# A fused attention, router, expert and dense kernel: routing chains interleaved, branch hints, one exit branch

## Chip, cores and metric

The kernel runs on one core of a Trainium2 chip. The metric is the device time of one execution in microseconds (us). Beside it stands one execution taken by the hardware profiler, whose trace gives every duration here. TensorE (PE in the rows; PEld is its weight load), VectorE (DVE), ScalarE (ACT), GpSimd (POOL) and SyncE (SP) each run their own list of instructions in order; a "q" behind a name (PEldq, ACTq) is that engine's sequencer with its branches, semaphores and register loads.

## What is computed

```python
# attention with pooled queries: b=4, h=8, 1152 keys of 64; 576 queries, each the mean of two
scores = scale * q_pool @ k^T;  p = exp(scores - max);  x = (p / sum(p)) @ v      # x: 2304 x 512
# routed experts: 8, top-1, for tokens whose skip score is above 0
do_compute = x @ w_skip > 0
e_idx = argmax(xc @ w_gate);  gate_w = softmax(xc @ w_gate)[e_idx]
for e in range(8):
    y[e_idx == e] = gate_w * (relu(xc @ w1[e]) @ w2[e])       # 512 -> 1024 -> 512
x[do_compute] += y
# dense layer, 512 -> 2048 -> 512
h = x @ w_in;  out = (h - tanh(h)) @ w_out
```

With the inputs used, four of the eight experts get tokens, 618, 476, 56 and 2 of them.

## The kernel before

**Stages.** Attention runs to about 449 us, the routing of the last tokens to about 467, the expert stage to about 640, and the dense layer fills the rest. Nothing is reordered by a scheduler: each engine runs its instructions in the order in which the code issues them.

**Routing** (`Router.route`). The tokens lie in 18 tiles of 128 (NT); the first 13 are counted during the attention, and `route` finishes the last five. On VectorE it issues three chains of small operations, one behind the other. The first, lines 652 to 668, counts tokens per expert (`n`), turns them into tiles of 128 slots (`nt`), ranks the experts by tokens (`rnk`, `mt`) and writes `perm`, a table by rank: number of tiles, expert, first slot tile. Lines 669 to 677 then work out `last` (the last slot tile), `few` (whether dense weights are left to load because experts have few tiles) and `more`, which holds for each rank its number of tiles, plus 2NT if the next rank has none. The second chain, `rank` (lines 600 to 611), gives each token its place within its expert. The third, lines 682 to 685, adds the expert's first slot and writes `sg16`, an f16 copy. `invert` compares `sg16` with slot numbers and multiplies on TensorE, which gives `inv`, the token that stands in each slot; the first gather of tokens (`fetch`, line 845, an indirect transfer issued by GpSimd) reads it. The first expert's weights (`load`, line 836, also GpSimd) need only `perm`, which the engine reads into registers (`reg`, line 819; the register load is called TENSOR_LOAD).

**Experts** (`Experts`). The counts are known on the chip only, so the code holds for rank a as many copies of a tile as it could need: 18, 9, 6, 5, 4, 3, 3, 3. `place(a)` stands in `If(n > 0)` (line 938), runs tile 0, then `chain(1)`, in which each further tile is nested in `If(n > j)` (line 945), then `place(a + 1)`. So every engine meets one compare per tile, and behind an expert's last tile each jumps over the copies that are left. On the side that is not taken it adds the semaphore counts which the skipped instructions would have added (EVENT_SEMAPHORE rows; INC_SWDGE_SEM on GpSimd), and goes on. With these inputs ranks 0 to 3 have 5, 4, 1 and 1 tiles and ranks 4 to 7 none. Behind rank 3 the engines therefore jump twice: out of its chain (line 945) and over `place(4)` (line 938).

**A tile** (`tile(a, j, base)`). TensorE multiplies 96 times into the hidden layer (line 889, 128x128), transposes the next tile's tokens (line 865), and multiplies 24 times back (128x512). ScalarE and VectorE split float32 into f16 pairs (lines 850, 851), make the hidden activations (904, 905); ScalarE copies the result of the tile before (`evac`, line 869), GpSimd stores it (874) and gathers the next tokens (845). In an expert's last tile `If(self.end <= j + 1)` (line 925) splits the first part of the next expert's weights; `self.end` is `more` in a register of ScalarE and VectorE. Behind the stage stand `dense.fetch_y` (line 1024, two gathers by GpSimd), the last `evac` and `store`, and `dense.first` (line 1041).

**Zeros.** The rows `ys` that hold the experts' results are filled with zeros during the attention, by six transfers on SyncE's queue: five of 1280 KB and one of 256 KB, in `on_pair`.

Of the kernel before, what the change touches and what calls it, by code (L numbers as in the profile page):

```python
# [13 lines left out]
I32 = mybir.dt.int32  # L14
# [475 lines left out]
class Router:  # L490
# [4 lines left out]
    def __init__(self, ctx, tc, w_skip, w_gate, x_all, ident32, ov):  # L495
# [8 lines left out]
        self.r7, self.slot, self.inv = t("r7", [P, 2, NT]), t("slot", [P, NT], I32), t("inv", [P, CAP + 2], I32)  # L504
        self.more, self.perm = t("more", [P, 2, E], I32), t("perm", [P, 3, E], I32)
        self.cnt, self.gate, self.last, self.least = t("cnt", [P, E]), t("gate", [P, NT]), t("last", [P, 1]), t("least", [P, E])
        self.iom, self.iota, self.tv = t("iom", [P, 1, E]), t("iota", [P, 1, P]), t("tv", [P, NT])
# [128 lines left out]
    def route(self, ps_pool, tag):  # L636
        nc, e = self.nc, self.EARLY
        T = lambda n, s, dt=F32: self.wk1.tile(s, dt, name=n)
        V = nc.vector
        S88 = [P, E, E]  # L640
        for f in self.pick(e, NT):
            f()
        before, all_ = self.count(e, NT, ps_pool.tile([P, 512], F32, tag=tag, name="ps_r"))
        n, n1 = T("n", [P, E]), T("n1", [P, E], I32)
        key, rk, base = T("key", [P, E]), T("rnk", [P, E]), T("base", [P, E])
        vals = T("vals", [P, 3, 1, E], I32)
        perm = T("permf", [P, 3, E])
        cmp, bt, mt, mm = T("cmp", S88), T("bt", S88), T("mt", S88), T("mm", [P, 3, E, E])
        few, last, so, sl = T("few", [P, 1]), self.last, T("so", [P, NT, E]), T("sl", [P, NT])
        iota8 = self.iota[:, 0, 0:E]  # L650
        nt = vals[:, 0, 0]
        V.tensor_copy(vals[:, 1, 0], iota8)
        V.tensor_tensor(out=n, in0=all_, in1=self.cnt, op=ALU.add)
        V.tensor_scalar(out=n1, in0=n, scalar1=float(P - 1), scalar2=None, op0=ALU.add)
        V.scalar_tensor_tensor(out=key, in0=n, scalar=float(E), in1=iota8, op0=ALU.mult, op1=ALU.subtract)
        V.tensor_scalar(out=nt, in0=n1, scalar1=7, scalar2=None, op0=ALU.logical_shift_right)
        V.tensor_tensor(out=cmp, in0=key.unsqueeze(1).to_broadcast(S88), in1=key.unsqueeze(2).to_broadcast(S88),
                        op=ALU.is_gt)
        V.tensor_tensor(out=bt, in0=cmp, in1=nt.unsqueeze(1).to_broadcast(S88), op=ALU.mult)
        V.tensor_reduce(out=rk, in_=cmp, axis=AX.X, op=ALU.add)  # L660
        V.tensor_reduce(out=base, in_=bt, axis=AX.X, op=ALU.add)
        V.tensor_tensor(out=mt, in0=rk.unsqueeze(1).to_broadcast(S88), in1=iota8.unsqueeze(2).to_broadcast(S88),
                        op=ALU.is_equal)
        V.tensor_copy(vals[:, 2, 0], base)
        V.tensor_tensor(out=mm, in0=vals.to_broadcast([P, 3, E, E]), in1=mt.unsqueeze(1).to_broadcast([P, 3, E, E]),
                        op=ALU.mult)
        V.tensor_reduce(out=perm, in_=mm, axis=AX.X, op=ALU.add)
        V.tensor_copy(self.perm, perm)
        V.tensor_reduce(out=last, in_=nt, axis=AX.X, op=ALU.add)
        V.tensor_tensor(out=perm[:, 1], in0=perm[:, 0], in1=self.least, op=ALU.is_lt)  # L670
        V.tensor_scalar(out=perm[:, 2, 0:E - 1], in0=perm[:, 0, 1:E], scalar1=0.0, scalar2=2.0 * NT,
                        op0=ALU.is_equal, op1=ALU.mult)
        V.tensor_reduce(out=few, in_=perm[:, 1], axis=AX.X, op=ALU.max)
        V.tensor_tensor(out=self.more[:, 1, 0:E - 1], in0=perm[:, 0, 0:E - 1], in1=perm[:, 2, 0:E - 1], op=ALU.add)
        V.tensor_scalar(out=last, in0=last, scalar1=1.0, scalar2=1.0, op0=ALU.max, op1=ALU.subtract)
        V.tensor_copy(self.more[:, 0, 1:2], few)
        V.tensor_copy(self.more[:, 0, 0:1], last)
        for f in self.rank(e, NT, before):
            f()
        for t in range(e, e + 3):  # L680
            self.row(t)
        V.tensor_tensor(out=so, in0=base.unsqueeze(1).to_broadcast([P, NT, E]), in1=self.oh, op=ALU.mult)
        V.tensor_reduce(out=sl, in_=so, axis=AX.X, op=ALU.add)
        V.tensor_tensor(out=self.r7[:, 1], in0=self.r7[:, 1], in1=sl, op=ALU.add)
        V.tensor_copy(self.sg16, self.r7[:, 1])

# [39 lines left out]
class Wide:  # L726
# [43 lines left out]
    def parts(self, i):  # L770
# [7 lines left out]
        else:  # L778
            nc.scalar.copy(dh, a)
        nc.gpsimd.tensor_tensor(out=dl, in0=a, in1=dh if dh.dtype == F16 else dh.bitcast(F32), op=ALU.subtract)  # L780


class Experts:
# [381 lines left out]
def pooled_attention__moe__tanhshrink_kernel(ctx, tc, q, k, v, moe_w_skip, moe_w_gate, moe_w1, moe_w2,  # L1165
# [8 lines left out]
    with tc.manual_schedule():  # L1174
# [7 lines left out]
        with ExitStack() as actx:  # L1182
# [5 lines left out]
            def on_pair(b, c):  # L1188
# [10 lines left out]
                if b == 0:  # L1199
                    for i in range(c, 6, 4):  # L1200
                        n = 5 if i < 5 else 1
                        todo.append(lambda i=i, n=n: nc.sync.dma_start(
                            out=ys[i * 5 * P:(i * 5 + n) * P].rearrange("(a p) d -> p a d", p=P),
                            in_=zero.unsqueeze(1).to_broadcast([P, n, DM])))
                return todo
# [12 lines left out]
        with ExitStack() as bctx:  # L1218
# [47 lines left out]
```

## Time and profile before

| | us |
|---|---|
| median of 3 runs | 1045.09 (1044.58 to 1046.73) |
| the profiled execution | 1046.08 |
| its span, first to last instruction | 1044.6 |
| TensorE busy in the span | 941.9 (90%) |
| VectorE, ScalarE, GpSimd busy | 788.5, 641.4, 557.1 |
| granted clock of TensorE, mean | 0.962 of full |

The 1.5 us between the profiled execution and its span lie around the instructions. Times within the kernel are counted from the span's start. Busy time is that of computing and data-moving instructions; a branch or a register load is not busy, but has rows of its own, in which its duration holds whatever it waited for. Idle time in brackets stands ahead of an instruction, with what ended it.

### The profile page before, as it was taken

How to read it: one execution, taken by the hardware profiler on the slowest of the kernel's cores; microseconds unless marked ns; L12 is line 12 of the kernel's file. 1: busy time of each engine (PE TensorE's matmuls, PEld its weight loads, DVE VectorE, ACT ScalarE, POOL GpSimd, SP SyncE). 2: the span in 40 equal slices, each digit the busy share in tenths (PEclk: the TensorE clock that was granted, in tenths of full speed). 3: DMA queues.
4: the chain of work that ended last, by engine and by line, in shares of the span. 5: the costliest groups of instructions: out<-in, count | busy, mean ns of one | idle time of the engine just before them, and what ended most of it. 6: DMA issues, size and time to landing. Idle time of an engine off the chain costs nothing. (4 is left out here: it accounts for less than half of the span.)

```text
span 1044.6 us, 25445 instructions
## 1 busy us (share of the span) xinstructions
PE 941.9 (90%) x10249; PEld 704.6 (67%) x10249; DVE 788.5 (75%) x1420; ACT 641.4 (61%) x1211; POOL 557.1 (53%) x491
## 2 busy tenths in 40 slices
PE   5689999999999999939878775999999999999998
PEld 2355666666666666637656543778888888888886
DVE  8678889888889998768979762867666666666654
ACT  4587999888999998835463451444444444444443
POOL 8847998888899986524646411342332223322221
PEclk8889999999999999969989887999999999999999
DMA  7765878666666720169657433121111211212100
GB/s 222 147 157 177 213 190 206 139 134 126 162 143 127 166 59 15 28 224 330 215 180 261 150 126 136 31 72 41 46 56 31 72 41 46 56 32 71 21 21 21
DMA packets 129796, 122.52 MB, mean 117 GB/s; under 512 B 92270, under 2 KB 96878, under 8 KB 128622
## 3 DMA queue, kind: packets, MB, share of 16 engines
q1 hardware_dynamic: 121934, 92.74, 34.7%
q0 software_dynamic: 7712, 27.79, 7.9%
q8 instruction: 92, 1.51, 0.6%
q14 instruction: 58, 0.48, 0.1%
HBM read 74.73 MB, written 19.14 MB: 90 GB/s over the span
## 5 line engine op out<-in xcount | busy, mean ns | idle before, releaser
L242 POOL TENSOR_TENSOR pl<-p,ph 128x512 f16<-128x512 f32 x214 | 263.8, 1252 | 59.5 <-ACT p L237 45.1
L188 DVE TENSOR_REDUCE m<-ps_m 128x1 f32<-128x384 f32 x432 | 225.5, 548 | 37.4 <-PE ps_m L187 34.7
L1095 POOL TENSOR_TENSOR gl<-v,gh 128x512 fp32r<-128x512 f32 x71 | 92.9, 1308 | 270.7 <-ACT gh L1094 268.3
L236 ACT ACTIVATE ph<-ps_e 128x512 f16<-128x512 f32 x279 | 177.0, 635 | 57.5 <-PE ps_e L248 54.2
L299 PEld LDWEIGHTS <-ph 128*128 128x128 f16 x2304 | 133.4, 99 | 49.7 <-issue 22.6
L1094 ACT CAST gh<-v 128x512 fp32r<-128x512 f32 x72 | 44.5, 619 | 188.5 <-DVE v L1093 188.5
L1078 PE MATMUL ps_ch<-xT,wi 128*128 128x256 f16 x576 | 158.7, 275 | 0.7 <-ACT xT L1062 0.7
L1079 PE MATMUL ps_ch<-xT,wi 128*128 128x256 f16 x576 | 157.9, 274 | 1.1 <-DMA xT<-xs 0.8
L1080 PE MATMUL ps_ch<-xT,wi 128*128 128x256 f16 x576 | 157.9, 274 | 0.0
L187 PE MATMUL ps_m<-ks,qT 128*128 128x384 f16 (+1 forms) x480 | 122.7, 338 | 23.9 <-DVE m L188 16.1
L299 PE MATMUL ps_a<-vh,ph 128*128 128x65 f16 x1152 | 136.7, 195 | 0.0
L299 PE MATMUL ps_a<-vh,pl 128*128 128x65 f16 x1152 | 136.6, 195 | 0.0
L299 PE MATMUL ps_a<-vl,ph 128*128 128x65 f16 x1152 | 136.5, 195 | 0.0
L1089 DVE SCALAR_TENSOR_TENSOR v<-u,ps_ch 128x512 f32<-128x512 f32 x72 | 49.3, 685 | 114.4 <-ACT t L1087 108.9
L237 ACT ACTIVATE p<-ps_e 128x512 f32<-128x512 f32 x211 | 134.5, 637 | 0.0
L1111 PE MATMUL ps_co<-wo,gh 128*128 128x512 f32 x288 | 119.7, 416 | 0.0
L1113 PE MATMUL ps_co<-wo,gl 128*128 128x512 f32 x288 | 113.7, 395 | 1.5 <-POOL gl L1095 1.5
L247 PE MATMUL ps_e<-qT,ks 128*128 128x512 f16 x288 | 111.4, 387 | 2.6 <-DVE pl L242 1.8
L1112 PE MATMUL ps_co<-wo,gh 128*128 128x512 f32 x288 | 113.5, 394 | 0.0
L248 PE MATMUL ps_e<-qT,kh 65*128 65x512 f16 x288 | 111.8, 388 | 1.9 <-DMA qT<-mt 1.9
L299 PEld LDWEIGHTS <-pl 128*128 128x128 f16 x1152 | 108.4, 98 | 0.0
L187 PEld LDWEIGHTS <-qT 128*128 128x128 f16 (+1 forms) x480 | 42.9, 102 | 68.1 <-issue 34.3
(222 smaller groups left out, 2152.8 us busy)
## 6 DMA issues: line engine op xcount, KB each, us to landing
v<-in_v_dram SPq DMA_DIRECT2D x16, 576.0 KB
k<-in_k_dram SPq DMA_DIRECT2D x15, 576.0 KB
q<-in_q_dram SPq DMA_DIRECT2D x16, 512.0 KB
raw<-in_moe_w_in_dram SPq DMA_DIRECT2D x8, 1024.0 KB
w1f<-in_moe_w_dram POOLq DMA_DIRECT2D x8, 1024.0 KB, 7.6
w2f<-in_moe_w_dram POOLq DMA_DIRECT2D x8, 1024.0 KB, 8.3
raw<-in_moe_w_out_dram SPq DMA_DIRECT2D x8, 1024.0 KB
ys<-zero SPq DMA_DIRECT2D x5, 1280.0 KB
```

The costliest lines, as they stand in the source:

```text
L187: nc.tensor.matmul(ps[o, 0:384], w, ks[:, h, c * 384:(c + 1) * 384], start=True, stop=True)
L188: nc.vector.tensor_reduce(out=s["m2"][:, i, c:c + 1], in_=ps[:, 0:384], axis=AX.X, op=ALU.max)
L236: nc.scalar.activation(ph, ps, AF.Exp, scale=2.0 ** -20)
L237: nc.scalar.activation(src, ps, AF.Exp, scale=2.0 ** -20)
L242: (nc.vector if dve else nc.gpsimd).tensor_tensor(out=pl, in0=src, in1=ph, op=ALU.subtract)
L299: self.nc.tensor.matmul(o, x, r, start=first and i == 0, stop=k == NKT - 1 and i == 2, skip_group_check=True)
L1078: nc.tensor.matmul(ps[:, a], self.wi[0][:, w], xh[:, c], start=c == 0, stop=False)
L1079: nc.tensor.matmul(ps[:, a], self.wi[0][:, w], xl[:, c], start=False, stop=False)
L1080: nc.tensor.matmul(ps[:, a], self.wi[1][:, w], xh[:, c], start=False, stop=c == 3)
L1111: nc.tensor.matmul(o, gh[:, a, s], self.wo[0][:, w], start=f == 0, stop=False)
L1112: nc.tensor.matmul(o, gh[:, a, s], self.wo[1][:, w], start=False, stop=False)
L1113: nc.tensor.matmul(o, gl[:, a, s], self.wo[0][:, w], start=False, stop=f == 15)
```

## The change

Four things change. In `route`, the three chains become lists of operations, and the first two are issued in turn, one of each; the last step of the first chain (`mm`, `permf`, `perm`) is issued in turn with the third. The eight operations for `last`, `few` and `more` become `tails`, issued behind `invert`. The 256 KB of zeros are issued by GpSimd behind the attention. In the expert stage `tile` issues, where the expert may have one more tile, a hint to all engines on whether `n > j + 1`, tied to the branch of that tile by a label; one more hint goes to the branch on `few` behind the stage. And `self.end` is loaded by all five engines, with a new `If(self.end != 2 * NT + 1)` around `chain(1)` and `place(a + 1)`: it is not entered where the expert has one tile and the next has none.

```diff
@@ Router.route
+        place = [
+            lambda: V.tensor_tensor(out=n, in0=all_, in1=self.cnt, op=ALU.add),
...
+            lambda: V.tensor_copy(vals[:, 2, 0], base)]
+        order = [
+            lambda: V.tensor_tensor(out=mm, in0=vals.to_broadcast([P, 3, E, E]),
...
+            lambda: V.tensor_copy(self.perm, perm)]
+        slots = [
+            lambda: V.tensor_tensor(out=so, in0=base.unsqueeze(1).to_broadcast([P, NT, E]), in1=self.oh, op=ALU.mult),
...
+            lambda: V.tensor_copy(self.sg16, self.r7[:, 1])]
...
+        rank = self.rank(e, NT, before)
+        for i, f in enumerate(place):
+            f()
+            if i < len(rank):
+                rank[i]()
...
+        for i, f in enumerate(slots):
+            f()
+            if i < len(order):
+                order[i]()
+
+    def tails(self):
...
-        for f in self.rank(e, NT, before):
-            f()
@@ Experts
-    def tile(self, a, j, base):
+    def tile(self, a, j, base, n):
         nc = self.nc
+        if j + 1 < self.MOST[a]:
+            self.tc.mark_branch_hint_location("t%d_%d" % (a, j + 1), hint=n > j + 1, engines=ALL)
...
-                self.end = self.reg(self.more[:, 1], a, 3 * NT, (T.Activation, T.DVE))
+                self.end = self.reg(self.more[:, 1], a, 3 * NT, ALL)
...
-                    with tc.If(n > j):
-                        self.tile(a, j, base)
+                    with tc.If(n > j, label="t%d_%d" % (a, j)):
+                        self.tile(a, j, base, n)
                         chain(j + 1)
-            self.tile(a, 0, base)
-            chain(1)
-            self.place(a + 1)
+            self.tile(a, 0, base, n)
+            with tc.If(self.end != 2 * NT + 1) if a + 1 < E else ExitStack():
+                chain(1)
+                self.place(a + 1)
...
+        self.tc.mark_branch_hint_location("few", hint=few, engines=T)
...
-        with self.tc.If(few > 0):
+        with self.tc.If(few > 0, label="few"):
@@ on_pair, behind att.run() and behind invert
-                    for i in range(c, 6, 4):
-                        n = 5 if i < 5 else 1
+                    for i in range(c, 5, 4):
...
+            nc.gpsimd.dma_start(out=ys[25 * P:26 * P], in_=zero)
             router.route(att.ps_mx, "mx")
...
             router.invert(ps_i)
+            router.tails()
```

**VectorE, in `route`, from the copy of perm on, before.** Line 668 writes the table that GpSimd loads; 669 to 677 are the eight operations on `last`, `few` and `more`; 600 to 604 begin `rank`.

```order
L668 CAST perm<-permf 128x24
L669 TENSOR_REDUCE last<-vals 128x1
L670 TENSOR_TENSOR permf<-permf,least 128x8
L671 TENSOR_SCALAR permf<-permf 128x7
L673 TENSOR_REDUCE few<-permf 128x1
L674 TENSOR_TENSOR more<-permf 128x7
L675 TENSOR_SCALAR last<-last 128x1
L676 CAST more<-few 128x1
L677 CAST more<-last 128x1
L600 TENSOR_TENSOR off_10413<-ps_r,cnt 128x40
L603 TENSOR_TENSOR off_10413<-off_10413,oh 128x40
L604 TENSOR_REDUCE rf_10416<-off_10413 128x5
```

The same place in the changed kernel, where 612 ends `rank`, 666 to 669 are the order table, 671 to 674 the slots and 707 to 715 belong to `invert`:

```order
L612 TENSOR_TENSOR r_87<-r_87,kf_10396 128x5
L664 CAST vals<-base 128x8
L671 TENSOR_TENSOR so<-base,oh 128x144
L666 TENSOR_TENSOR mm<-vals,mt 128x192
L672 TENSOR_REDUCE sl<-so 128x18
L668 TENSOR_REDUCE permf<-mm 128x24
L673 TENSOR_TENSOR r_87<-r_87,sl 128x18
L669 CAST perm<-permf 128x24
L674 CAST sg_86<-r_87 128x18
L707 TENSOR_TENSOR by<-iota_105,sg_86 128x450
L616 TENSOR_SCALAR pick_110<-iota_105,r_87,tv 128x128 x2
L715 TENSOR_SCALAR inv<-ps_i 128x25
```

The copy of perm moved from ahead of `rank` to just ahead of the f16 copy `sg`, and the eight operations are out of the row.

**TensorE, end of rank 0's tile 0 and start of its tile 1, before.** LDWEIGHTS is the weight load ahead of each matmul.

```order
L889 LDWEIGHTS bhid
L889 MATMUL ps_by<-w2s_10480,bhid 128x512
L945 COMPARE_AND_BRANCH
L889 LDWEIGHTS w1s_10478
L889 MATMUL ps_bh<-bxt_105,w1s_10478 128x128
```

The same place in the changed kernel (946 is the test on `end` in the tile, 970 the new branch around the chain, 966 the branch to the next tile, 902 and 1285 the hint):

```order
L910 LDWEIGHTS bhid
L910 MATMUL ps_by<-w2s_10472,bhid 128x512
L946 COMPARE_AND_BRANCH
L946 UNCONDITIONAL_BRANCH x2
L970 COMPARE_AND_BRANCH
L966 COMPARE_AND_BRANCH
L902 REGISTER_ALU
L1285 BRANCH_PREFETCH_HINT
L910 LDWEIGHTS w1s_10470
L910 MATMUL ps_bh<-bxt_108,w1s_10470 128x128
```

Between the two tiles one compare became three compares and two branches, and tile 1 now begins with a register operation and the hint. The hint that `tile(0, 0)` calls for is not among TensorE's rows: in the built program hints stand from an expert's tile 1 on, since that of tile 0 belongs to a branch which lies inside the new one.

## Rows read from the trace of the kernel before

**Rows 1.** Busy time by stage: us, busy (count) of each engine, PEclk, DMA, GB/s.
```profile
530.00:550.00 20.00, 15.15 (x130) 11.39 (x131) 13.81 (x21) 12.23 (x22) 7.33 (x8) 0.83 0.61 198
586.00:605.00 19.00, 13.53 (x127) 10.15 (x128) 13.16 (x20) 11.34 (x22) 7.59 (x8) 0.82 0.45 150
605.00:640.00 35.00, 18.18 (x136) 11.55 (x134) 14.52 (x25) 10.77 (x21) 4.75 (x6) 0.80 0.31 97
640.00:1044.00 404.00, 395.20 (x2600) 322.59 (x2600) 259.87 (x413) 181.22 (x317) 113.49 (x90) 0.99 0.17 50
```

**Rows 2.** TensorE's timeline: start, us, line, operation, count [idle before <-releaser].
```profile
518.00 2.33 PE L889 MATMUL ps_by<-w2s,bhid 128*128 128x512 f16 x10 [1.83 <-DVE bhid L905]
520.17 5.52 PE L889 MATMUL ps_bh<-bxt,w1s 128*128 128x128 f16 x96
...
530.27 2.33 PE L889 MATMUL ps_by<-w2s,bhid 128*128 128x512 f16 x10 [1.11 <-DVE bhid L905]
537.18 8.26 PE L889 MATMUL ps_bh<-bxt,w1s 128*128 128x128 f16 x96 [4.58 <-ACTq L945]
...
593.80 7.29 PE L889 MATMUL ps_bh<-bxt,w1s 128*128 128x128 f16 x96 [5.33 <-DVE w1s L851]
...
612.05 0.90 PE L889 MATMUL ps_bh<-bxt,w1s 128*128 128x128 f16 x7 [5.33 <-PEq L945]
615.11 6.50 PE L889 MATMUL ps_bh<-bxt,w1s 128*128 128x128 f16 x89 [2.16 <-issue]
...
635.57 2.08 PE L1041 MATMUL ps_i<-by,pick 128*128 128x512 f32 x2 [8.33 <-ACTq L975]
```

**Rows 3.** Line 945, 530 to 540 us: count, min/median/max ns, first and last start.
```profile
L945 PEldq COMPARE_BRANCH  x2: 192/3124/6057, 530.3 to 536.6; - x2
...
L945 DVEq EVENT_SEMAPHORE  x1: 21/21/21, 535.8 to 535.8; - x1
```

**Rows 4.** The same view of line 945, 584 to 596 us.
```profile
L945 PEldq COMPARE_BRANCH  x2: 323/1912/3502, 586.2 to 593.2; - x2
...
L945 DVEq EVENT_SEMAPHORE  x1: 21/21/21, 591.0 to 591.0; - x1
```

**Rows 5.** The same view of line 945, 604 to 614 us.
```profile
L945 PEldq COMPARE_BRANCH  x1: 5903/5903/5903, 605.7 to 605.7; - x1
```

**Rows 6.** The same view of line 945, 622 to 640 us.
```profile
L945 PEldq COMPARE_BRANCH  x1: 3457/3457/3457, 626.2 to 626.2; - x1
```

**Rows 7.** The same view of line 938, 622 to 640 us.
```profile
L938 POOLq EVENT_SEMAPHORE  x6: 17/30/43, 630.9 to 631.3; - x6
...
L938 PEldq COMPARE_BRANCH  x2: 197/2521/4845, 629.9 to 635.1; - x2
```

**Rows 8.** DMA queues, 607 to 616 us: TensorE's instruction queue, packets, MB, share.
```profile
q8 instruction: 3, 0.05, 2.1%
```

**Rows 9.** VectorE's timeline in the routing.
```profile
456.55 0.18 DVE L668 CAST perm<-permf 128x24 int32<-128x24 f32 x1
...
457.38 0.19 DVE L600 TENSOR_TENSOR off<-ps_r,cnt 128x40 f32<-128x40 f32 x1
...
459.72 0.18 DVE L685 CAST sg<-r 128x18 f16<-128x18 f32 x1
```

**Rows 10.** Timelines of GpSimd, ScalarE and TensorE behind the routing.
```profile
458.61 0.97 POOL L836 DMA_DIRECT2D w1f<-in_moe_w_dram  x1 [13.70 <-DVE kf L608]
...
462.21 1.04 POOL L845 DMA_INDIRECT bx<-xd,inv  x1 [2.50 <-DVE slot L700]
...
635.90 0.97 POOL L1024 DMA_INDIRECT cy<-ys,slot  x1 [11.86 <-issue]
...
466.30 1.15 ACT L850 ACTIVATE w1s<-w1f 128x512 f16<-128x512 f32 x2 [3.18 <-DMA w1f<-in_moe_w_dram]
...
467.04 1.09 PE L865 MATMUL ps_bt<-ident,bx 128*128 128x128 f32 x4 [2.10 <-DMA bx<-xd,inv]
```

**Rows 11.** Line 819, register loads, whole span.
```profile
L819 PEldq TENSOR_LOAD <-perm x5: 301/312/494, 464.3 to 617.5; - x5
```

More of the change, by code (lines that the diff above doesn't have):

```diff
@@ L505, in __init__ @@
         self.more, self.perm = t("more", [P, 2, E], I32), t("perm", [P, 3, E], I32)
+        self.vals, self.permf, self.few = t("vals", [P, 3, 1, E], I32), t("permf", [P, 3, E]), t("few", [P, 1])
         self.cnt, self.gate, self.last, self.least = t("cnt", [P, E]), t("gate", [P, NT]), t("last", [P, 1]), t("least", [P, E])
@@ L645, in route @@
         key, rk, base = T("key", [P, E]), T("rnk", [P, E]), T("base", [P, E])
-        vals = T("vals", [P, 3, 1, E], I32)
-        perm = T("permf", [P, 3, E])
+        vals, perm = self.vals, self.permf
         cmp, bt, mt, mm = T("cmp", S88), T("bt", S88), T("mt", S88), T("mm", [P, 3, E, E])
-        few, last, so, sl = T("few", [P, 1]), self.last, T("so", [P, NT, E]), T("sl", [P, NT])
+        so, sl = T("so", [P, NT, E]), T("sl", [P, NT])
         iota8 = self.iota[:, 0, 0:E]
         nt = vals[:, 0, 0]
-        V.tensor_copy(vals[:, 1, 0], iota8)
@@ L653, in route @@
[L653 to L666, printed above, removed]
@@ L667, in route @@
-        V.tensor_reduce(out=perm, in_=mm, axis=AX.X, op=ALU.add)
-        V.tensor_copy(self.perm, perm)
-        V.tensor_reduce(out=last, in_=nt, axis=AX.X, op=ALU.add)
+        place = [
+            lambda: V.tensor_tensor(out=n, in0=all_, in1=self.cnt, op=ALU.add),
+            lambda: V.tensor_scalar(out=n1, in0=n, scalar1=float(P - 1), scalar2=None, op0=ALU.add),
+            lambda: V.scalar_tensor_tensor(out=key, in0=n, scalar=float(E), in1=iota8, op0=ALU.mult, op1=ALU.subtract),
+            lambda: V.tensor_scalar(out=nt, in0=n1, scalar1=7, scalar2=None, op0=ALU.logical_shift_right),
+            lambda: V.tensor_tensor(out=cmp, in0=key.unsqueeze(1).to_broadcast(S88),
+                                    in1=key.unsqueeze(2).to_broadcast(S88), op=ALU.is_gt),
+            lambda: V.tensor_tensor(out=bt, in0=cmp, in1=nt.unsqueeze(1).to_broadcast(S88), op=ALU.mult),
+            lambda: V.tensor_reduce(out=rk, in_=cmp, axis=AX.X, op=ALU.add),
+            lambda: V.tensor_reduce(out=base, in_=bt, axis=AX.X, op=ALU.add),
+            lambda: V.tensor_tensor(out=mt, in0=rk.unsqueeze(1).to_broadcast(S88),
+                                    in1=iota8.unsqueeze(2).to_broadcast(S88), op=ALU.is_equal),
+            lambda: V.tensor_copy(vals[:, 2, 0], base)]
@@ new lines, in route @@
+        V.tensor_copy(vals[:, 1, 0], iota8)
+        rank = self.rank(e, NT, before)
[3 more added lines that the diff above has]
+                rank[i]()
+        for f in rank[len(place):]:
+            f()
+        for t in range(e, e + 3):
+            self.row(t)
+        for i, f in enumerate(slots):
+            f()
+            if i < len(order):
+                order[i]()
+    def tails(self):
+        V, vals, perm, few, last = self.nc.vector, self.vals, self.permf, self.few, self.last
+        V.tensor_reduce(out=last, in_=vals[:, 0, 0], axis=AX.X, op=ALU.add)
@@ L672, in route @@
                         op0=ALU.is_equal, op1=ALU.mult)
+        V.tensor_scalar(out=last, in0=last, scalar1=1.0, scalar2=1.0, op0=ALU.max, op1=ALU.subtract)
         V.tensor_reduce(out=few, in_=perm[:, 1], axis=AX.X, op=ALU.max)
         V.tensor_tensor(out=self.more[:, 1, 0:E - 1], in0=perm[:, 0, 0:E - 1], in1=perm[:, 2, 0:E - 1], op=ALU.add)
-        V.tensor_scalar(out=last, in0=last, scalar1=1.0, scalar2=1.0, op0=ALU.max, op1=ALU.subtract)
+        V.tensor_copy(self.more[:, 0, 0:1], last)
         V.tensor_copy(self.more[:, 0, 1:2], few)
-        V.tensor_copy(self.more[:, 0, 0:1], last)
-        for f in self.rank(e, NT, before):
-            f()
[L680 to L685, printed above, removed]
     def invert(self, ps_pool):
@@ L780, in parts @@
         nc.gpsimd.tensor_tensor(out=dl, in0=a, in1=dh if dh.dtype == F16 else dh.bitcast(F32), op=ALU.subtract)
+ALL = tuple(getattr(mybir.EngineType, n) for n in ("PE", "Activation", "Pool", "DVE", "SP"))
 class Experts:
```

10 lines of the change are left out of this document (7 added, 3 removed).

## The prediction

> **What bounds the kernel now.** I read first the busy time by stage. In the last stage, from 640 us on, TensorE is busy 395.20 of 404 us; nothing that the change touches stands there. In the expert stage there are holes: TensorE is busy 15.15 of 20 us, 13.53 of 19 us and 18.18 of 35 us in the three stretches in which one expert ends and the next begins, and the granted clock is 0.83, 0.82 and 0.80 there [rows 1]. Then TensorE's timeline. With these inputs the four experts that get tokens have 5, 4, 1 and 1 tiles, and so there are four exits, where the rest of an expert's tiles is jumped over. I call them A (expert rank 0 to 1), B (1 to 2), C (2 to 3) and D (out of the stage). The reader is to look at the brackets: TensorE is idle for 4.58, 5.33, 5.33 and 8.33 us, and after C again for 2.16 us that nothing explains but "issue" [rows 2]. That is 25.7 us. What ends it is a sequencer, not data: in the row of the compare that guards the next tile, TensorE's sequencer stands for 6.06 us at A, 3.50 at B, 5.90 at C and 3.46 at D, and at D for 4.85 us more at the branch over the next expert [rows 3 to 7], though the shortest compare of that sequencer at A took 0.19 us [rows 3]. At C three 16 KB packets of TensorE's instruction queue lie beside it [rows 8]: the code behind the jump is not there and has to be brought. So a taken jump costs 3.5 us where little is in its way, and about 6 where something is.
>
> [...]
>
> **Part 1, routing on VectorE.** The rank chain and the placement chain are now issued in turn, so an operation no longer stands directly behind the one whose result it needs. Today perm is cast at 456.55 us (done 456.73), the eight operations on last, few and more fill the time up to 457.38, where rank begins, and the slots' f16 copy starts at 459.72 [rows 9]. The eight go behind the inversion, where VectorE waits for the first weights until about 466 (cover: the 3.18 us for which ScalarE waits for them, up to 466.30 [rows 10]); without that cover they cost their 0.65. Taking the spaces between operations from the same rows, 0.1 to 0.13 us for an independent one and the duration plus 0.03 for a dependent one, the f16 copy comes at about 457.5, 2.2 us sooner. But perm's cast now stands just ahead of it, behind nine operations of rank and three of slots that it stood ahead of: about 457.55 instead of 456.73, so 0.8 later. Two paths hang on these. The gather of the first tokens (issued 462.21, then the wait of 2.10 us up to 467.04) follows the f16 copy; POOL's loads of perm and the first weight transfer (458.61) follow perm, and ScalarE waits for that transfer until 466.30 [rows 10]. One gets sooner by at most 1.6 us, the other later by 0.8; the split of the weights has 0.7 us in hand to the transposes at 467.04. Ends: -1.0 and +0.8. I take **-0.3**.
>
> **Part 2, the 256 KB of zeros.** It leaves SyncE's queue and is issued by POOL behind the attention, ahead of its loads of perm. One issue costs POOL about 0.97 us, by the row of the first weight transfer [rows 10]. The cover: POOL's idle time of 13.70 us before that transfer, in the same row. **0**; without the cover +1.
>
> **Part 3, one wait more on each engine.** "end" was loaded by ScalarE and VectorE, now by all five, and the test on it is now a branch on each engine in every tile. A load is 0.31 us on TensorE [rows 11], one for each expert; it lies in the shadow of matmuls in flight, since the sequencer reached its compare at 530.3 while the matmuls before it ended at 532.60 [rows 2, 3]: 2.3 us in hand. At C, with one tile, half of it may show. In each tile come a compare, two branches, a register operation and a hint, at 0.02 us (adding a count on VectorE) to 0.19 (the shortest compare on TensorE) each [rows 3]: 0.1 to 1.0 us a tile, which TensorE has in hand and VectorE and ScalarE have in part in their waits for TensorE. Over eleven tiles 0 to 1.0 shows in the end; by the lower price, which is VectorE's, I take **+0.4**.
>
> **Part 4, the hints, exits A and B.** A hint stands at the start of each tile but an expert's first; it carries whether the next tile is there. Seven run here: one each in the last tile of ranks 0 and 1, and five in tiles that are followed by another. No row of before shows the instruction. Bounds: it does nothing (the compare stays at 6.06 and 3.50), or the target is there before the jump. What is late next is then VectorE, which is still splitting the next expert's weights: its counts are added at 535.8 at A and at 591.0 at B [rows 3, 4], and the next expert's first matmul waits for all engines. So A starts at 535.85 instead of 537.18: -1.3. The gap is then 3.25 us. A gap of 1.83 us left the clock alone (96 matmuls in 5.52 us, 2.4 GHz), behind one of 4.58 they took 8.26 [rows 2], 2.74 more; 3.25 lies between, nearer to the longer by a hair. So A gives -1.3 to -4.1, and I take **-1.5**. B starts at 591.05 instead of 593.80: **-2.7**; of B's own clock loss, 7.29 against 5.52, I take nothing back.
>
> **Part 5, exit C.** Ranks 2 and 3 have a single tile, and a first tile has no hint, so here the jump stays unaided. But code moves: a tile on TensorE is four instructions longer. At C the sequencer stood 5.90, and after seven matmuls (14 instructions with their weight loads) it stood again for 2.16 [rows 2, 5]: target and line end lay close together. Exits B and D, with 3.50 and 3.46 [rows 4, 6], are what a jump costs without that. Ends: 0 (unchanged) and -2.4 - 2.16 = -4.6. The four more instructions in each of the tiles ahead shift the place by tens, past the 14, so I take nearly all of it, less the load of "end": **-4.0**. [...]
>
> **Part 6, exit D.** Two jumps in a row, 3.46 and 4.85 [rows 6, 7], become one. If the one costs 3.5, TensorE is out 4.85 sooner, and with it ScalarE's last copy. POOL too adds its counts twice today, the second time at 631.3, and issues the gather of y at 635.90 only [rows 7, 10]; with one fetch instead of two that is some 4.2 us sooner. The later of the two decides: **-4.2** (-3 to -5; the one jump could cost 6).
>
> **Sum:** -0.3 + 0 + 0.4 - 1.5 - 2.7 - 4.0 - 4.2 = -12.3 us. The profiled execution took 1046.08 us, so 1033.8; it lies 1.0 over the median of 1045.09, from which it would be 1032.8. I say 1033.
>
> **Rivals.**
> Hints without effect. They take their answer from a register, and nothing shows that this kind acts. A stays; at B the second hold (compare left at 589.7, matmul at 593.80) may still go with the shift of code, so -2.7 to -1.6; C and D stay: -12.3 + 1.5 + 0.5 = -10.3, 1034.8. Chance 0.17.
> The code's position is not the cause at C, or the shifted code has a line end in another bad place: -12.3 + 4.0 = -8.3, 1036.8. Chance 0.14.
> The hinted code takes the room of the code that comes next in order. Then the exit tiles stop inside the tile: two more fetches of 3.5 [rows 4], -12.3 + 7.0 = -5.3, 1039.8. Chance 0.10. For it: at C a jump cost more with another fetch beside it. [...]
> Slower: every hint, whichever way it points, makes the sequencer fetch anew at the next line end. All seven hinted tiles then pay 3.5: -12.3 + 24.5 = +12.2, 1057.3. It decides from 12.3/7 = 1.8 us a tile on. Against it: for five of the seven the code asked for is the code that comes next anyway. Chance 0.11.
> The later weights eat the routing's gain and jumps are bound by something unseen, so that only 0 to 2 us are left: about 1044. Chance 0.05.
>
> **How the numbers follow.** My forecast has 0.43; with its own ends it is 1028 (A keeps the clock, C and D at their best) to 1036. The other faster cases reach to 1040. The range 1028 to 1042 leaves out the slower case and half of the small one, some 0.15, and a few hundredths below. About 0.2% (2 us) is what a measurement of this kernel can tell from no change: faster by more than that 0.43 + 0.17 + 0.14 + 0.10 = 0.84, same 0.05, slower 0.11.
>
> **What would show it.** In the changed kernel's trace: at A and B the long compare rows on TensorE's sequencer are gone and the first matmul comes within 0.2 us of VectorE's counts; at C about 3.5 instead of 5.90, and no 2.16 behind seven matmuls; at D one long row, not two. The f16 copy near 457.5, the first weight transfer near 459.4. Idle time in the middle of tiles would prove me wrong on the hints; long rows left at A would make them inert.

## The result

The changed kernel takes 1030.72 us (median of 4 runs, 1030.27 to 1031.87), the kernel before 1044.84 beside it: a ratio of 0.9863, 95% interval 0.9841 to 0.9885. The forecast was 1033, with a range of 1028 to 1042; the time lies in it, 2.3 us under the forecast. The profiled execution took 1031.87 us, its span is 1030.4, and the mean granted clock rose from 0.962 to 0.971.

TensorE's timeline of the changed kernel, to be read against [rows 2] (start, duration, operation, count, idle time before it and what ended it):

```profile
518.14 5.52 PE L910 MATMUL ps_bh<-bxt,w1s 128*128 128x128 f16 x96
...
528.23 2.33 PE L910 MATMUL ps_by<-w2s,bhid 128*128 128x512 f16 x10 [1.11 <-DVE bhid L926]
534.85 7.05 PE L910 MATMUL ps_bh<-bxt,w1s 128*128 128x128 f16 x96 [4.29 <-ACTq L966]
...
587.63 5.52 PE L910 MATMUL ps_bh<-bxt,w1s 128*128 128x128 f16 x96 [2.68 <-ACT w1s L869]
...
605.05 7.75 PE L910 MATMUL ps_bh<-bxt,w1s 128*128 128x128 f16 x96 [6.28 <-ACT w1s L869]
...
623.91 2.08 PE L1064 MATMUL ps_i<-by,pick 128*128 128x512 f32 x2 [5.49 <-ACTq L998]
```

The four exits now have gaps of 4.29, 2.68, 6.28 and 5.49 us, against 4.58, 5.33, 5.33 and 8.33. The stop of 2.16 us behind seven matmuls at C is gone (96 in one row), and behind B the 96 matmuls run in 5.52 us (granted clock 1.00) instead of 7.29 (0.74). So B gave most. A's gap hardly moved, C's grew, and D's fell by 2.84 us only. At 1.00 the f16 matmuls of the changed kernel follow each other by 0.216 us at 512 columns and by 0.0558 at 128, 0.160 us for 384 columns, 2.4 columns a ns; no run shows a clock in GHz, and the 2.4 GHz of the prediction stands for this rate alone.

The compares in front of the next tile, which now stand at line 966 and are to be read as [rows 3 to 5]; first exit A with the counts that each engine adds behind it, then B, then C:

```profile
L966 PEldq COMPARE_BRANCH  x2: 193/286/380, 528.7 to 530.8; - x2
L966 ACTq COMPARE_BRANCH  x2: 49/60/70, 529.5 to 534.9; - x2
...
L966 PEldq EVENT_SEMAPHORE  x1: 51/51/51, 530.6 to 530.6; - x1
L966 DVEq EVENT_SEMAPHORE  x1: 21/21/21, 533.7 to 533.7; - x1
L966 ACTq EVENT_SEMAPHORE  x1: 17/17/17, 534.8 to 534.8; - x1
```

```profile
L966 PEldq COMPARE_BRANCH  x2: 189/271/353, 583.1 to 585.1; - x2
...
L966 DVEq EVENT_SEMAPHORE  x1: 21/21/21, 587.5 to 587.5; - x1
```

```profile
L966 PEldq COMPARE_BRANCH  x1: 5968/5968/5968, 598.2 to 598.2; - x1
```

At A and B TensorE's compare takes 0.38 and 0.35 us instead of 6.06 and 3.50. At C it still takes 5.97. At A TensorE is through at 530.6 and VectorE at 533.7; it is ScalarE that adds its counts last, at 534.8, and TensorE starts at 534.85.

A single profile has scatter of its own: the routing's first operation on the new counts (line 653) starts at 454.30 us in the profile of before and at 453.63 in that of the changed kernel, and between 450.26 and 454.87 in those below, though little ahead of it differs (one transfer; in e11 and e13 the padding at the start). The dense stage takes 400.8 to 403.8 us in them. So I also compare the stretch between, from line 653 to the dense layer's first transposes: 186.48 us before, 175.24 after, 11.24 less.

### The profile page after: what moved, and what is told of

Its sections match the earlier page's. It is cut to its first block, busy times and chain, and to the rows that moved or that the text cites. A ratio compares the mean times of both kernels' runs of the same rounds, so it can differ in the third digit from the quotient of the medians.

```text
span 1030.4 us, 25577 instructions
## 1 busy us (share of the span) xinstructions
PE 936.9 (91%) x10249; PEld 701.2 (68%) x10249; DVE 788.4 (77%) x1420; ACT 641.3 (62%) x1211; POOL 558.6 (54%) x492
```

## The experiments

Each ran beside the kernel before on its own chip, where that took 1043.07 to 1045.38 us (median); the ratio is to that. "Stretch" is the one just defined, from the one profile.

| kernel | us, median | ratio (95%) | stretch, us |
|---|---|---|---|
| before | 1044.84 | 1 | 186.48 |
| changed | 1030.72 | 0.9863 (0.9841 to 0.9885) | 175.24 |
| e1 no hints | 1032.28 | 0.9868 (0.9848 to 0.9888) | 179.99 |
| e2 routing alone | 1044.24 | 0.9980 (0.9963 to 0.9996) | 188.73 |
| e3 hint in first tiles, no exit branch | 1036.87 | 0.9913 (0.9889 to 0.9937) | 180.03 |
| e4 rank 3's second weights cut | 1030.70 | 0.9847 (0.9824 to 0.9871) | 173.77 |
| e5 before, 32 instructions of padding | 1037.66 | 0.9938 (0.9914 to 0.9961) | 179.49 |
| e7 e3 and a hint on the next expert's branch | 1036.81 | 0.9931 (0.9912 to 0.9951) | 179.31 |
| e8 hints on TensorE alone | 1030.80 | 0.9883 (0.9858 to 0.9908) | 176.07 |
| e9 a hint on the exit branch too | 1033.36 | 0.9896 (0.9857 to 0.9935) | 175.42 |
| e10 all of rank 3's weights cut | 1028.68 | 0.9859 (0.9841 to 0.9877) | 173.10 |
| e11 changed, 186 instructions of padding | 1031.19 | 0.9865 (0.9820 to 0.9910) | 175.88 |
| e12 changed, 16 activations of padding | 1030.85 | 0.9872 (0.9833 to 0.9911) | 175.66 |
| e13 changed, 130 instructions of padding | 1038.46 | 0.9939 (0.9923 to 0.9954) | 183.94 |

My theory was the prediction's: hints bring A and B, the shift of the code brings C, one jump for two brings D. The rivals: hints without effect, and a place of the code that is not the cause.

### e1: no hints

```diff
-        if j + 1 < self.MOST[a]:
-            self.tc.mark_branch_hint_location("t%d_%d" % (a, j + 1), hint=n > j + 1, engines=ALL)
...
-        self.tc.mark_branch_hint_location("few", hint=few, engines=T)
```

> The changed kernel without any hint (labels stay). Theory 1, the hints bring TensorE's target code before the jump: its compare goes from 0.38 back to about 6 us at exit A and from 0.35 to about 3.5 at B. What the time does then depends on what is next late: at A ScalarE adds its counts at 534.8 anyway, 528.7 + 6 gives the same; at B 583.1 + 3.5 = 586.6 lies ahead of VectorE's 587.5. So +0.3 to +2 us (1031 to 1033), with 0.6 of it from the hint on few. Theory 2, the hints do nothing and the shorter compares come from the shifted code: compares stay at 0.4 and the time at 1030.7.

Line 964 (the compare) at A, then at B, and TensorE's timeline:

```profile
L964 PEldq COMPARE_BRANCH  x2: 188/3101/6014, 525.9 to 532.1; - x2
...
L964 ACTq EVENT_SEMAPHORE  x1: 17/17/17, 532.5 to 532.5; - x1
```

```profile
L964 PEldq COMPARE_BRANCH  x2: 179/1914/3648, 582.2 to 586.1; - x2
...
L964 DVEq EVENT_SEMAPHORE  x1: 21/21/21, 586.6 to 586.6; - x1
```

```profile
532.98 8.11 PE L908 MATMUL ps_bh<-bxt,w1s 128*128 128x128 f16 x96 [5.13 <-ACTq L964]
...
587.16 8.32 PE L908 MATMUL ps_bh<-bxt,w1s 128*128 128x128 f16 x96 [3.03 <-ACT w1s L869]
```

The hints do act on TensorE: without them its compare is back at 6.01 and 3.65 us. But they decide nothing much. At A ScalarE's counts come at 532.5, half a microsecond behind TensorE's; at B TensorE is held until 585.9 and VectorE until 586.6. The gaps are 5.13 and 3.03 us instead of 4.29 and 2.68, and the ratios, 0.9868 and 0.9863, can't be told apart. The stretch is 4.75 us longer; of that 8.11 - 7.05 + 8.32 - 5.52 = 3.9 us are the clock behind A and B, which the gap alone does not set (e3 had 2.47 us at B and 7.15 for the 96 matmuls). The profiled execution is the slowest of e1's four, and its granted clock, 0.964, is the lowest (0.969 to 0.970 in the others), so part of this is its own. So: hints 0 to 4.7 us. B's shorter gap is there without them, 3.03 instead of 5.33; the faster matmuls behind it are not in this execution (8.32 us), but they are in e5, which has no hint either.

### e2: the routing alone

The edits are those of `route`, `tails` and the zeros; no hint, no new branch, `end` on two engines.

> The routing part alone (chains in turn, the eight operations later, 256 KB of zeros on GpSimd); expert stage as before. By the trace of the changed kernel the first transposes stand 0.76 us nearer to the start of the routing: 1044.0, and nothing changes at A to D. If the later copy of perm costs, 1044.8 or more; if the dense stage's 2.3 us or the wait of 1.83 us in tile (0,4) came from here too, 1041 to 1042.

From line 653 to the first expert matmul it took 13.81 us, against 14.51 before and 13.75 in the changed kernel: 0.7 us. The ratio gives 0.4 to 3.9 us. The exits are those of before; B, then C:

```profile
591.93 7.26 PE L908 MATMUL ps_bh<-bxt,w1s 128*128 128x128 f16 x96 [5.50 <-DVE w1s L870]
...
611.34 0.90 PE L908 MATMUL ps_bh<-bxt,w1s 128*128 128x128 f16 x7 [6.53 <-PEq L964]
614.40 7.55 PE L908 MATMUL ps_bh<-bxt,w1s 128*128 128x128 f16 x89 [2.15 <-issue]
```

The 5.50 and the stop of 2.15 behind seven matmuls are there again: the routing takes neither away. The stretch of this one profile is 2.2 us longer than that of before, though the ratio is below 1: C's compare took 7.03 us here instead of 5.90, and the 89 matmuls 7.55 instead of 6.50.

### e3: a hint in first tiles too, no exit branch

```diff
-            with tc.If(self.end != 2 * NT + 1) if a + 1 < E else ExitStack():
-                chain(1)
-                self.place(a + 1)
+            chain(1)
+            self.place(a + 1)
```

> The changed kernel without the new branch around the chain, so that the hint of an expert's first tile is issued too and exit C is hinted; end on two engines as before. If a hint serves C as it serves B: TensorE's compare at C 0.4 instead of 5.97 us, the first matmul of rank 3 follows VectorE's counts (601.5), about 3 us sooner; at D the second jump (4.85 on TensorE) is back, +1.2 to +4: in all 1029 to 1032. If a hint with one tile's lead is too short or is lost: C stays at 6, and with D's second jump 1034 to 1035.

TensorE's compare at C, and its timeline from there:

```profile
L966 PEldq COMPARE_BRANCH  x1: 455/455/455, 601.3 to 601.3; - x1
```

```profile
603.83 5.52 PE L910 MATMUL ps_bh<-bxt,w1s 128*128 128x128 f16 x96 [1.34 <-ACT w1s L869]
611.67 1.09 PE L884 MATMUL ps_bt<-ident,bx 128*128 128x128 f32 x4 [2.32 <-DMA bx<-xd,bix]
612.76 8.15 PE L910 MATMUL ps_by<-w2s,bhid 128*128 128x512 f16 x24
627.35 2.08 PE L1063 MATMUL ps_i<-by,pick 128*128 128x512 f32 x2 [6.44 <-ACTq L997]
```

As foreseen C's compare falls to 0.46 us, the gap to 1.34, and the clock stays up (5.52 us instead of 7.75). Little of it is left in the end: rank 3's tile then waits 2.32 us for its gather, and the 24 matmuls take 8.15 us (granted clock 0.67) instead of 5.34 (1.00); from the end of rank 2's matmuls to the end of rank 3's 18.42 us remain of 19.65. D is two jumps again: from there to the dense layer's first transposes 13.42 us instead of 10.45. The time is 5 to 6 us worse than the changed kernel's; I had allowed 1029 to 1032. Of the stretch's 4.8 us more, 3.0 are D's, and 1.3 lie in the routing, within its scatter. What the jump at C no longer hid was the arrival of rank 3's data.

### e4 and e10: less traffic at exit C

Ahead of the weights' transfer in `load`, for the second weights in e4; e10 has `if a == 3:`.

```diff
+                if (a, i) == (3, 1):
+                    o, x = o[:, 0:1, 0:64], x[:, 0:1, 0:64]
```

> The changed kernel, but of rank 3's second weights only a corner of 64 columns is loaded (the rest is what lies there), so that no bulk transfer runs at exit C. Theory 1, the jump at C takes 5.97 instead of 3.5 us because the instruction fetch stands behind bulk transfers (the 16 DMA engines were 99% busy from 594 to 604 us): compare about 3.5, first matmul of rank 3 about 2.4 us sooner, 1028. Theory 2, it is the place of the code: the code is the same, so 5.97 stays and the time with it, but for the waits on those weights.

> The changed kernel, but of all of rank 3's weights only corners are loaded (the rest is what lies there), so that but for a gather and a store of 256 KB nothing runs on the DMA engines at exit C. Theory 1, the fetch behind the jump waits for bulk transfers: TensorE's compare at C falls from 5.97 (5.31 with the second weights cut, where the first were still under way) to about 3.5. Theory 2, the place of the code, which is the same here: 5 to 6 stays.

The DMA engines in the changed kernel from 594 to 604.5 us (busy tenths in 40 slices, then the queue that carries the weights: packets, MB, share of 16 engines), the same queue and TensorE's instruction queue (q8) in e10 during its compare at C, 598.1 to 602.0 us, and the compare at C in e4 and in e10:

```profile
DMA  9999999645698899999999997999577999998999
...
q0 software_dynamic: 913, 3.42, 97.5%
```

```profile
q0 software_dynamic: 143, 0.33, 39.9%
...
q8 instruction: 1, 0.02, 1.4%
```

```profile
L968 PEldq COMPARE_BRANCH  x1: 5313/5313/5313, 597.8 to 597.8; - x1
```

```profile
L968 PEldq COMPARE_BRANCH  x1: 3902/3902/3902, 598.1 to 598.1; - x1
```

TensorE's code is the same in all three. With the queue at 97.5% the compare takes 5.97 us, with the second weights cut 5.31, with all cut 3.90. That alone would be thin, since the full weights gave 4.40 in e12, with TensorE's code the same. But the traces have the packet of code itself. One 16 KB packet of TensorE's instruction queue falls into each of these compares: it starts 3.59 us after the compare in the changed kernel, 2.71 in e4 and 1.45 in e10, lasts 0.9 to 1.2, and the compare ends 1.4 to 1.6 behind it. In the kernels with full weights it is the first part too that varies: 1.93 in e12, 2.22 in e11 (compare 4.76), 3.98 in e1 (6.49), 5.45 in e9 (7.92). So the long jump at C is the fetch of code waiting for bulk transfers, and the price depends on where in the burst the jump falls. The whole time does not show it: the ratios of e4 and e10 lie in the interval of the changed kernel, and the 1028 us expected of e4 did not come (1030.70).

### e5: the kernel before, moved by 32 instructions

```diff
+        for i in range(16):
+            self.nc.tensor.matmul(ps[:, 300:301], self.ones, self.tri[:, 0:1], start=True, stop=True)
```

> The kernel before, with 16 tiny matmuls (32 instructions with their weight loads) more on TensorE while it waits for the first tokens, so that all of the experts' code lies 32 places later. Theory 1, the stop of 2.16 us after seven matmuls at exit C and the second hold at B (compare left at 589.7, first matmul at 593.80) come from where the code's 16 KB pieces end: both go, first matmul of rank 2 within 0.3 us of VectorE's counts, 2.7 + 2.2 = 4.9 us sooner in all, 1040; A and D as before. Theory 2, they come from the jump or the traffic alone: both stay, 1045.

TensorE at B, C and D:

```profile
589.79 5.52 PE L891 MATMUL ps_bh<-bxt,w1s 128*128 128x128 f16 x96 [2.67 <-ACT w1s L852]
...
607.68 7.69 PE L891 MATMUL ps_bh<-bxt,w1s 128*128 128x128 f16 x96 [6.74 <-PEq L947]
...
629.02 2.08 PE L1043 MATMUL ps_i<-by,pick 128*128 128x512 f32 x2 [8.03 <-ACTq L977]
```

Sixteen matmuls that do nothing make the kernel before 0.4 to 0.9% faster, 6 us. B's gap is 2.67 us, just that of the changed kernel, without a hint; the stop at C is gone; D is as before. C's compare took 7.27 us here, beside the same weights. The gain is larger than the 4.9 us expected at B and C, since the matmuls behind A and B ran faster too, 7.15 and 5.52 us instead of 8.26 and 7.29.

### e11 and e13: the changed kernel, moved

Ahead of the attention; e13 has 65 in place of 93.

```diff
+        with tc.tile_pool(name="pad", bufs=1, space=PSUM) as pp:
+            pad = pp.tile([P, 512], F32, name="pad")
+            for i in range(93):
+                nc.tensor.matmul(pad[:, 0:1], ident, ident[:, 0:1], start=True, stop=True)
```

> The changed kernel with 93 tiny matmuls (186 instructions with their weight loads) more on TensorE at the very start, while it waits for its first data; that puts the experts' targets back to where the kernel before had them within the 16 KB pieces of code, 18 instructions ahead of a piece's end at C. Theory 1, the place of the code gave 5 to 6 us of the change: the stop after some seven matmuls at C comes back (2.2) and a hold of 2.7 at B behind the hinted compare, 1035 to 1036. Theory 2, the exit branch and the hints gave it, and place matters in the kernel before only: 1030.7.

e11 measured 1031.19 and no stop: the forecast failed, since I had counted the place from rank 0's chain, not from the chains left at B and C. The two traces give the length of a piece: in the first 450 us 49 packets of 16 KB on TensorE's instruction queue stand beside 12474 matmuls and weight loads, 255 to a packet. By the right count, an estimate, e11's targets stand 30 to 40 behind a piece's start (e13's stop at C, below, puts its target there some 18 ahead of a piece's end, and e11 has 56 instructions more), and no stop came there; as a test it says nothing. The right distance was then tried:

> The changed kernel with 65 tiny matmuls (130 instructions) more on TensorE at the very start. The 186 of the run before were counted from rank 0's chain; counted from the chains that are left at B and C they put the targets 30 to 40 behind a piece's start, a harmless place, so that run did not test the place. With 130 the code that A, B and C jump to stands where rank 2's stood at C in the kernel before: 18 instructions ahead of a piece's end, the next expert's matmuls 16 ahead. Theory 1, the place of the code decides: at C TensorE stops again after seven matmuls for about 2.2 us; at A and B, where TensorE is there 4 and 2 us before the matmuls may start, the next piece has time to come, so 0 at A and 0 to 1 at B; time 2 to 3.5 us over the changed kernel. Theory 2, place matters in the kernel before only: no stop, 1030.7.

TensorE at B, C (two rows) and D, and its compares at D (line 970):

```profile
587.65 6.86 PE L910 MATMUL ps_bh<-bxt,w1s 128*128 128x128 f16 x96 [2.67 <-ACT w1s L869]
...
606.77 0.90 PE L910 MATMUL ps_bh<-bxt,w1s 128*128 128x128 f16 x7 [6.64 <-ACT w1s L869]
610.03 7.20 PE L910 MATMUL ps_bh<-bxt,w1s 128*128 128x128 f16 x89 [2.36 <-issue]
...
630.06 2.05 PE L1064 MATMUL ps_i<-by,pick 128*128 128x512 f32 x2 [7.21 <-issue]
```

```profile
L970 PEldq COMPARE_BRANCH  x2: 3474/3680/3885, 622.1 to 626.4; - x2
```

It stops again behind seven matmuls at C, for 2.36 us, with a packet of code at 607.2 to 607.6, and not at A or B, just as counted. At D there are now two long compares, 3.47 and 3.89 us, which I had not foreseen; a 16 KB packet of code falls into each, at 623.6 to 624.0 and at 626.4 to 626.8, and by the same count, an estimate, a piece ends between the exit's counts and what follows them. In all the kernel is 7.7 us slower for code that computes nothing, where I had expected 2 to 3.5: the stop is 2.36, D's gap 1.72 longer, and 2.4 more are the 96 matmuls behind A and B (8.12 and 6.86 us instead of 7.05 and 5.52), of which it is not shown that they go with the place. Place decides in the changed kernel as in the one before.

### e7 and e9: more hints

e7 is e3 with a second hint in an expert's first tile, behind the load of the next expert's count:

```diff
+                    self.tc.mark_branch_hint_location("p%d" % (a + 1), hint=self.tiles > 0, engines=ALL)
```

e9 is the changed kernel with a hint ahead of an expert's first tile:

```diff
+                tc.mark_branch_hint_location("x%d" % a, hint=self.end != 2 * NT + 1, engines=ALL)
```

> The hints in every tile, an expert's first too, without the new branch, and one more hint in an expert's first tile on the branch to the next expert; so C has a hint, and D has one on each of its two jumps. If TensorE holds two hinted targets: compares of 0.4 us at C and twice at D (D's second was 3.41 with the first alone), and what then ends D is GpSimd's two jumps: 1033 to 1036. If the second hint pushes the first out: a compare of 3.5 or more at C, and 1038.

> The changed kernel with one more hint in each expert's first tile, on the new branch that leaves the stage, so that exit D is hinted (12 us ahead). If TensorE alone holds D: its compare falls from 3.63 to 0.4 there, but ScalarE adds its counts at 620.6 and starts its last copy at 623.26 by its own fetches, so 0 to -0.5 us, 1030.5. If the hint serves ScalarE and GpSimd too: D's gap falls from 5.49 towards 2, -2 to -3, 1028. If it pushes out something that A or B needs: slower by 1 to 3.

e7 at C, then e9 at D, TensorE and ScalarE, and TensorE's timeline from C:

```profile
L967 PEldq COMPARE_BRANCH  x1: 6472/6472/6472, 600.5 to 600.5; - x1
```

```profile
L972 ACTq COMPARE_BRANCH  x2: 49/60/70, 620.8 to 621.5; - x2
L972 ACTq EVENT_SEMAPHORE  x2: 17/17/17, 621.3 to 621.4; - x2
L972 PEldq COMPARE_BRANCH  x2: 189/284/378, 622.0 to 623.3; - x2
```

```profile
609.14 8.19 PE L910 MATMUL ps_bh<-bxt,w1s 128*128 128x128 f16 x96 [8.72 <-ACT w1s L869]
...
624.54 1.13 PE L1066 MATMUL ps_i<-by,pick 128*128 128x512 f32 x2 [1.58 <-ACTq L1000]
```

In e7 the later hint cost the earlier one its effect: 6.47 us at C, where e3 had 0.46 with one. In e9 the exit's compare takes 0.38 us and D's gap is 1.58 instead of 5.49. Here the hint served ScalarE as well: it adds its counts 0.5 us after its compare (620.8 to 621.3), against 4.1 in the changed kernel (616.5 to 620.6) and 2.4 to 2.9 in the seven others with the exit branch. But C's compare took 7.92 and its gap 8.72. I did not separate whether that is the traffic or the hint; the packet of code that started 5.45 us after the compare, with the weights' queue at 95.9% up to there, speaks for the traffic. The time is not better, 1033.36, where 1028 was expected if ScalarE was served too.

### e8 and e12: the other engines

e8 gives the tiles' hints to TensorE alone (`engines=ALL[0:1]`); e12 adds 16 activations on ScalarE while it waits for the first weights.

> The changed kernel with the tiles' hints on TensorE alone. Theory 1, only TensorE's hints bring anything (ScalarE adds its counts 5.3 us after its compare at A with hints and 6.2 without): 1030.7 as with all, less some 0.1 us a tile for the instructions saved. Theory 2, the other engines' hints serve A and B: ScalarE or VectorE adds its counts later there by 2 us or more, 1033.

> The changed kernel with 16 tiny activations more on ScalarE, while it waits for the first weights, so that its experts' code lies 16 places later. Theory 1, ScalarE's late counts at exit A (compare at 529.5, counts at 534.8, its own last work done at 531.3) are a fetch for a piece of code that ends near the jump's target: moved by 16, the counts come at 531.4 or at another place's cost, A's gap falls from 4.29 to some 3.2 (VectorE at 533.7) and the time by 1 to 3. Theory 2, it is the fetch for the jump itself, which the hint does not spare ScalarE: unchanged, 1030.7.

e8 is 0.9883, within the interval of the changed kernel; ScalarE's counts at A come 5.9 us after its compare (5.3 with hints on all, 6.2 without any). So the other engines' hints serve neither A nor B. In e12 they come 4.8 us after it; the kernels with hints on all engines scatter from 4.8 to 6.1 there, so that moving by 16 changed nothing that can be told. What ScalarE waits for at A, for some 3.5 us after its own last operation, stays open. A fetch of its own is likely, as at D, where e9's hint took it away, but at A it was not shown, and a hint did not spare it there.

## Why the prediction held, and where its steps did not

**What bounds the kernel.** Right: 11.2 of the 14.2 us between the two spans lie between the routing and the dense layer, most of it at the exits; the rest is within the scatter named above.

**Routing, -0.3.** The steps came out as worked out. From line 653 the f16 copy starts 3.16 us on instead of 5.42 (2.26 sooner, forecast 2.2), the first weights are issued 5.12 on instead of 4.31 (0.81 later, forecast 0.8):

```profile
456.70 0.18 DVE L669 CAST perm<-permf 128x24 int32<-128x24 f32 x1
456.79 0.17 DVE L674 CAST sg<-r 128x18 f16<-128x18 f32 x1
```

```profile
458.75 0.83 POOL L855 DMA_DIRECT2D w1f<-in_moe_w_dram  x1 [13.84 <-DMA raw<-in_moe_w_in_dram]
...
459.89 1.05 POOL L864 DMA_INDIRECT bx<-xd,inv  x1 [0.20 <-issue]
...
464.73 1.15 ACT L869 ACTIVATE w1s<-w1f 128x512 f16<-128x512 f32 x2 [4.34 <-DMA w1f<-in_moe_w_dram]
```

To be read as [rows 9, 10]. The net was -0.8 (first expert matmul 13.75 us behind line 653 instead of 14.51), not -0.3: the weights landed 5.98 us after their issue instead of 7.69, so the later issue cost nothing, and the gather was issued 1.65 us sooner (6.26 from line 653 instead of 7.91). The profiles scatter here: the first matmul comes 13.65 to 15.71 us after line 653 in kernels with the same routing. So the size rests on e2's ratio, 0.4 to 3.9 us, which has the zeros in it too. Their term of 0 fits the row of the first weight transfer, which still has 13.84 us of idle time ahead of it; they were not tried alone.

**A, -1.5.** The size was right, the step was not. I had taken VectorE as the next late, from [rows 3]; it is there at 533.7, and the hint made TensorE early, but ScalarE's counts came at 534.8. I had not looked where ScalarE's own came in the trace of before; it was behind TensorE and VectorE there too, and [rows 2] names it (ACTq) as what ended A's gap:

```profile
L945 ACTq EVENT_SEMAPHORE  x1: 17/17/17, 537.1 to 537.1; - x1
```

The gap gave 0.29 and the clock behind it 8.26 - 7.05 = 1.21, so that the size came out was luck. Nor does the length of the gap tell the clock, as I took it to: at B the 96 matmuls took 5.52 us behind gaps of 2.48 and 2.67 (e7, e5), and 7.15 and 6.86 behind 2.47 and 2.67 (e3, e13).

**B, -2.7.** The gap gave 5.33 - 2.68 = 2.65, as forecast, but not by the hint. The step that failed is "the target is there before the jump" as the cause: e5 has the same 2.67 without a hint. What had held B was the second fetch, between the jump's target and the next compare: in the trace of before a 16 KB packet of code starts at 590.76, behind TensorE's counts at 589.8 and ahead of its next compare at 593.2. I had named that only under the rivals. The clock kept at B, 1.77 us, was not in the sum.

**C, -4.0.** The term was mis-sized: 605.05 - 598.77 = 6.28 instead of 5.33, then no stop of 2.16, and 96 matmuls in 7.75. In all C gave 0.9 us. I had split the 5.90 of [rows 5] into 3.5 for the jump and the rest for the end of a piece of code nearby. e13 and e5 show that the place makes the 2.16; e4, e10 and the packets of code show that the rest of the 5.90 is a wait behind bulk traffic, which the change leaves.

The place itself is an estimate, from the 255 instructions to a packet and from where the stop comes. The runs agree with it: 32 instructions take the stop away, and 130 bring it back behind the same seven matmuls.

**D, -4.2.** It gave 2.84 at TensorE, 3.1 up to the dense layer's first transposes. TensorE's one compare is 3.63 us, as forecast; the later step is ScalarE's:

```profile
L970 ACTq COMPARE_BRANCH  x2: 38/44/50, 616.5 to 620.7; - x2
L970 PEldq COMPARE_BRANCH  x2: 190/1908/3625, 617.7 to 621.7; - x2
...
L970 ACTq EVENT_SEMAPHORE  x2: 17/17/17, 620.6 to 620.7; - x2
...
623.26 0.60 ACT L888 ACTIVATE by<-ps_by 128x512 f32<-128x512 f32 x1 [6.85 <-issue]
```

Its counts are added at 620.7, and its last copy, which TensorE waits for, starts only at 623.26, with nothing but "issue" ahead of it. From the end of the last expert matmul to the dense layer's first transposes it takes 13.36 to 13.56 us in the kernels with neither the branch nor a hint (before, e2, e5), and 8.72 (e1) to 10.45 (the changed kernel) in the seven with the branch and no hint on it, e13's bad place (12.51) left out. So the branch is worth 3 to 5 us at D, as forecast, and not always the same; the profile of the changed kernel is at the low end.

**Overhead, +0.4.** Not seen: rank 0's tiles 1 to 4 took 530.56 - 481.45 = 49.11 us, against 49.71; one wait in them alone, 1.83 us in [rows 2], fell to 1.10, so some 0.1 may have shown.

**The sum.** By ratios: routing alone 0.20%, the shift of the code 0.62% (e5), hints 0.05% (e1). Of 1.37% that leaves 0.50%, about 5 us, for the exit branch, which agrees with D; since each ratio is known to some 0.2%, it is known to some 0.4% only, and the branch was not tried without the shift that it brings. e2 and e1, beside the same runs of the kernel before, differ by the branch with its shift: 1.12%.

By the two profiles the stretch's 11.2 us are: routing 0.8, A 1.5, B 4.4, C 0.9, D 3.1, tiles 0.6. That the forecast of 12.3 came so near the 14.1 between the medians was partly luck: B gave 1.7 more than its term, C 3.1 and D 1.1 less, and some 3 us lie outside the stretch, in no term.

So the rival "hints without effect" was nearly right on the time for a wrong reason: the hints act, but at A and B something else is late. The rival "the position is not the cause at C" was right on the compare and wrong on the stop behind it, as e5 and e13 show. The two rivals in which a hint makes the tile stop are not seen: in all seven hinted tiles the 96 matmuls are one row of 5.52 us. And what is by these ratios the largest single part, the shift of TensorE's code, was in the prediction only as a side effect, under C and in the rival on hints.

## What to carry to other kernels

Where code is jumped over, look for each engine's own arrival behind the jump before you price a faster one: the last to add its counts sets the start (at A ScalarE at 534.8, for TensorE's 534.85). Before you credit an edit with a gain at a jump, move the code by a few dozen instructions and measure again; here that alone was worth 6 us in one direction and 8 in the other. A hint is worth giving where the compare is what is late and no bulk transfer is needed anyway behind the jump, one at a time (C's compare took 0.46 us in e3 with one, 6.47 in e7 with two).

## What the runs showed of the hardware

TensorE's jump to code that is not there costs 3.4 to 3.9 us in most jumps with the DMA engines 35% busy or less (3.50 at B and 3.46 at D before, 3.63 at D after, at 35, 10 and 23%; but 4.42 and 4.70 at D in e12 and e11) and 4.4 to 7.9 beside the full bulk weights; in the traces of before and after one 16 KB packet of code, or two (C before), falls into each long compare. What varies is how long the packet waits to start: 1.0 us at B before, 5.45 at C in e9. The second jump at D before, 4.85 us with the DMA engines 6% busy, does not fit this; two packets came there, and why stays open. With one hint, 12 to 13 us ahead, TensorE's jump costs 0.35 to 0.50; a second hint in the same tile undid the first (6.47 at C in e7). Where, by the count above, a jump's target lies some 18 instructions ahead of the end of a 16 KB piece, TensorE stops once more, 2.15 to 2.36 us (C in before, e2 and e13), but not where it waits there for others anyway (A and B in e13, 96 matmuls in one row behind gaps of 5.09 and 2.67). How much code TensorE holds no run here shows.
